# A larger fixed price for each VectorE instruction in the planner of a two-layer attention and S4D kernel, with later entries for the softmax inverses

## Chip, cores and metric

The kernel runs on one core of a Trainium2 chip. The metric is device time in microseconds (us) for one launch, as the median of several runs; for the kernel before it is 2675.46 us (three runs, 2673.86 to 2678.34).

## What is computed

The reference applies four residual layers to one sequence of 2048 rows of 640 float32 numbers: attention, S4D convolution, attention, S4D convolution, each with a layernorm in front, and with the same weights in both attentions and in both convolutions.

```python
def _A_ref(x, wqkv, wo):                      # 32 heads of 20
    q, k, v = split(x @ wqkv)
    p = softmax(einsum("bhqd,bhkd->bhqk", q, k) * 20 ** -0.5)
    return merge(einsum("bhqk,bhkd->bhqd", p, v)) @ wo

def _B_ref(u, log_A_real, A_imag, C_real, C_imag, log_dt, D_skip):
    ...
    K = 2.0 * einsum("dn,dnl->dl", C, exp(A * dt * pos)).real   # 640 x 2048, N = 128
    y = irfft(rfft(u_t, 4096) * rfft(K, 4096))[..., :2048]
    return y + u * D_skip

x = x + _A_ref(layernorm(x), ...);  x = x + _B_ref(layernorm(x), ...)   # twice
```

The convolution kernel K does not depend on x. It is built once, in pieces, beside the first attention, and used in both S4D layers.

## The kernel before

**Stages.** Attention 1 (its exponentials run from 116 to 1102 us of the span), its output projection and the transform of K, S4D 1, attention 2 (1491 to 2471 us), its output projection (2472 to 2523 us), S4D 2.

**A turn.** An attention goes through 32 turns: 8 groups g of 4 heads, and for each 4 blocks qb of 512 query rows. A turn walks over 16 tiles of 128 keys with two halves each, so it has 32 exponentials. `scores` (L851) issues eight small matmuls S (L858) into a PSUM tile of 128x1024 and one ScalarE exponential pt<-S; `values` (L884) issues eight matmuls pa (L892) for each key tile, which sum pt times V over the turn. V has a column of ones, so a row of each head's result is the softmax's sum. At a turn's last tile, `values` has VectorE copy pa0 into oc and add pa1 to it, and then multiply the oc of the turn before by db, the spread inverse of its sums (`scale`).

**The inverses.** Between a turn's end and that multiply, the sums go out to DRAM (dn<-oc, `sums`), come back spread over 128 partitions (dr<-dn, `load`), are inverted on VectorE (`invert`: a max and a reciprocal of 128x16), go out again (dn<-dr, `back`) and come back broadcast to all rows of a head (db<-dn, `spread`). These DMAs are issued from POOL's queue. Three more entries in the same list issue loads of kpw (DRAM to SBUF, also from POOL's queue), the tables from which K's next 32 channels are built.

**The filler.** `kgen` (L192 to L396) builds K. For each of 20 groups of 32 channels it has an expansion (28 small VectorE instructions on kpw, ktab, kwc, kwb, the last three of them ktab 128x896 and kdif 128x512), left parts (kat and ka, six VectorE instructions of 128x512) and right parts (kb), matmuls (L329) and evacuations of their sums (ko). Besides the filler there are jobs: projections to q and k (matmuls L611, evacuated by a group of five VectorE instructions qc, qc, sq, qhi, qlo) and to V (L577), a group of heads ahead. In the second attention there are pieces of its output projection instead of the filler (`rows_out`, L1040: pieces of three or two of a row's five tiles of 128, L1067), as many as fit; what is left of it is done after the attention by `out_proj` (L1286; matmuls L1307 and L1312).

**What sets the order.** The program is written out by a planner. `Plan` (L51) carries three running times, plan.pe, plan.act and plan.dve, while instructions are written. `Ordered.call` (L74) wraps every VectorE instruction: it adds a fixed part and elements/960 to plan.dve (which never stands more than 0.9 behind plan.pe), and ties the instruction behind the one written before it, so that VectorE's, POOL's and SyncE's (SP's) orders are those of the writing. Some decisions read these times:

- `fill` (L970), called for each exponential, first issues a tile's `values` when its exponentials are due, then jobs, then entries of `later` that are due, then filler.
- `weave` (L412) writes filler steps as long as plan.dve < plan.pe + 0.2.
- `emptied` (L404) puts an evacuation on VectorE not before plan.pe + 0.25, and marks the PSUM buffer free at plan.dve + 0.15; `slot` (L706) places a job's next matmuls only when its buffer is free.
- `later` is a list of (time, action): an action is issued when plan.pe has reached its time. The entries of the inverses are put at plan.dve plus an offset.
- `end_jobs` (L944) runs in the first turn in which the jobs are through; it finishes the filler and issues `prefetch` (L1147: the halves of wo, then x) from SP's queue.

So a VectorE instruction that is priced too low lets more filler be written ahead of the next evacuation than VectorE gets done by then; one that is priced too high holds filler back.

Of the kernel before, what the change touches and what calls it, by code (L numbers as in the profile page):

```python
# [62 lines left out]
class Ordered:  # L63
# [5 lines left out]
    def __getattr__(self, name):  # L69
        f = getattr(self.engine, name)  # L70
        if name not in ("dma_start", "memset", "partition_all_reduce", "activation", "copy") and not self.count:
            return f

        def call(out, *a, **k):  # L74
            if self.count:
                big = a[0].shape if "reduce" in name else out.shape
                self.plan.dve = max(self.plan.dve, self.plan.pe - 0.9) + 0.07 + math.prod(big[1:]) / 960
            made = f(out, *a, **k)  # L78
            if self.plan.keep:
                self.last = self.tie(made, self.last)  # L80
            elif self.floor is not None:
                self.tie(made, self.floor)
            return made
        return call
# [3 lines left out]
def mha_s4d_kernel(ctx, tc, x_in, wqkv, wo, lar, aim, cr, ci, ldt, dsk,  # L88
                   c_e1, c_eb, c_f2, c_fa, c_sel, c_lv, c_id, c_sg, c_e16, c_f16, c_id16, c_dn, out, parts="asas", general=None):
    nc = tc.nc  # L90
    plan = Plan()
# [97 lines left out]
    def chain(ins):  # L189
        last[0] = tie(ins, last[0])  # L190
# [208 lines left out]
    pend, slow = [], []  # L399
# [23 lines left out]
    def attention(x, stats):  # L423
# [100 lines left out]
        sqs, outs, later, ends = [[], []], [], [], [0.0, 0.0]  # L524
# [342 lines left out]
        def store_block(oc, blk):  # L867
            g, qb = divmod(blk, 4)
            for j in range(4):
                h = 4 * g + j  # L870
                ge.dma_start(ot[h * DH:(h + 1) * DH, 512 * qb:512 * qb + 512], oc[32 * j:32 * j + DH, :])
            stored[blk] = plan.pe

        def at_once(oc, blk):

            pb = pst("M", [P, 512], F32, tag="m0", name="m0")
            db = ev.tile([P, 512], F32, bufs=1, name="db")
            te.matmul(pb, dsel[0], oc, start=True, stop=True)
            ve.tensor_scalar_max(db, pb, 1e-30)
            ve.reciprocal(db, db)  # L880
            ve.tensor_mul(oc, oc, db)
            store_block(oc, blk)

        def values(qb, g, kt, pts, pa):  # L884

            V = Vt[g // 2 % 3]
            plan.on_pe(0.865)
            for r in range(2):
                rows = slice(64 * r, 64 * r + 64)
                for j in range(4):  # L890
                    h = 4 * (g % 2) + j
                    chain(te.matmul(pa[r][32 * j:32 * j + 32, :], V[rows, kt, VP * h:VP * h + 32],  # L892
                                    pts[j // 2][rows, 512 * (j % 2):512 * (j % 2) + 512],
                                    start=(kt == 0), stop=(kt == NI - 1), tile_position=(64 * r, 32 * j)))
            if kt == NI - 1:
                blk = 4 * g + qb
                oc = ev.tile([P, 512], F32, name="oc")
                dr = ev.tile([P, 16], F32, name="dr")
                db = []
                rows = dn[0, blk].rearrange("(j c) f -> j (c f)", j=4)  # L900
                plan.dve = max(plan.dve, plan.pe + 0.25)
                ve.tensor_copy(oc, pa[0])
                ve.tensor_add(oc, oc, pa[1])
                sums_[0] = plan.dve + 0.15
                while scaled:
                    scaled.pop(0)()
                if dsel and blk == NBK - 1:
                    later.append((plan.dve, lambda: at_once(oc, blk)))
                    return

                def sums():
                    for j in range(4):
                        ge.dma_start(rows[j:j + 1, :], oc[32 * j + DH:32 * j + DH + 1, :])

                def load():
                    ge.dma_start(dr, dn[0, blk])

                def invert():
                    ve.tensor_scalar_max(dr, dr, 1e-30)
                    ve.reciprocal(dr, dr)  # L920

                def back():
                    ge.dma_start(dn[1, blk], dr)

                def spread():
                    rows = dn[1, blk].rearrange("(j c) f -> j (c f)", j=4)
                    db.append(ev.tile([P, 512], F32, bufs=1, name="db"))
                    for j in range(4):
                        ge.dma_start(db[0][32 * j:32 * j + 32, :], rows[j:j + 1, :].to_broadcast([32, 512]))

                def scale():
                    ve.tensor_mul(oc, oc, db[0])
                    later.append((plan.dve + 0.3, lambda: store_block(oc, blk)))
                    later.sort(key=lambda e: e[0])
                later.extend((plan.dve + n, f) for n, f in (
                    (0.2, sums), (5.0, load), (10.0, invert), (11.0, back), (15.5, spread)))
                later.extend((plan.dve + n, lambda: slow and slow.pop(0)[1]()) for n in (18.0, 21.0, 24.0))
                if first_layer or g < H // 4 - 2:
                    scaled.append(scale)
                else:  # L940
                    later.append((plan.dve + 27.0, scale))
                later.sort(key=lambda e: e[0])
# [27 lines left out]
        def fill(j):  # L970

            if ready:
                t = max(ready[0][0] + 0.15, 0.0 if ready[0][3] else sums_[0])
                if t <= plan.pe + 0.1 or j and len(ready) > 2:
                    plan.on_pe(0.0, t)
                    values(*ready.pop(0)[1:])
            while slot(plan.act - 0.5):
                pass
            drain_later()
            weave()  # L980
# [146 lines left out]
        for r_ in ready:  # L1127
            values(*r_[1:])
# [574 lines left out]
```

## Time and profile before

| | |
|---|---|
| median of three runs | 2675.46 us (2673.86 to 2678.34) |
| profiled execution | 2680.85 us, its span 2679.1 us, mean granted TensorE clock 0.996 |
| TensorE (PE) busy | 2530.0 us, 94% |
| ScalarE (ACT) busy | 2368.7 us, 88% |
| VectorE (DVE) busy | 1516.0 us, 57% |
| GpSimd (POOL) busy | 827.7 us, 31% |
| 2048 exponentials pt<-S | 1928.6 us, 1032 ns each in the records, with ends that overlap the next one's start |
| exponentials of attention 1, first start to last end | 986 us |
| exponentials of attention 2 | 980 us |
| largest idle time of ACT before an exponential in attention 1 | 4.78 us, at 138.03 us |

In the prediction a row of the timeline reads: start, duration, engine, line, operation, out<-in, shapes, how many such instructions the row holds, and in brackets how long the engine stood idle before it and whose end it waited for. All VectorE and ScalarE instructions carry line 78 because the wrapper issues them; they are told apart by tile names. A row of the view by windows reads: window, its length, then the busy time and number of instructions on PE, PEld (weight load), DVE, ACT and POOL, then the granted clock as a share, the DMA share and GB/s. A row of grouped waits reads: engine, what waited, the releaser, and then us in total, number of times, longest.

### The profile page before, as it was taken

To read this page: it belongs to the slowest core of one execution; us is meant where nothing else is said; L and a number is where in the kernel's file an instruction comes from. 1 tells how busy PE (TensorE), PEld (TensorE's weight loads), DVE (VectorE), ACT (ScalarE), POOL (GpSimd) and SP (SyncE) were. 2 spreads that over 40 slices of the span, in tenths; PEclk is the share of its full clock that TensorE was granted. 3 is DMA by queue.
4 is the path that set the end of the run, shared out by engine and by line. 5 is a ranking of instruction groups with operands and counts; after the bars stand their busy time and mean duration, and the time that the engine had idled before them with its cause. 6 is when DMAs were issued, how large, how long until landed. Compare 5 with 4: busy or idle time off the path is not lost.

```text
span 2679.1 us, 116332 instructions
## 1 busy us (share of the span) xinstructions
PE 2530.0 (94%) x51106; PEld 1425.0 (53%) x51106; DVE 1516.0 (57%) x3451; ACT 2368.7 (88%) x2793; POOL 827.7 (31%) x1256
## 2 busy tenths in 40 slices
PE   7899999999999998899998999999999998999898
PEld 3445444444444443678896444454444443444788
DVE  8687777886855994477776333232233221154865
ACT  7889999999999999676655799999999999999564
POOL 1123323333323334301672122222222222222376
PEclk9999999999999999999999999999999999999999
DMA  6513222322221224364542121121121113222465
GB/s 210 181 49 86 67 76 55 87 55 76 52 61 49 54 68 155 110 233 162 189 151 69 40 59 50 50 58 47 45 65 38 54 30 93 69 67 60 145 190 162
DMA packets 186580, 242.18 MB, mean 90 GB/s; under 512 B 43376, under 2 KB 128976, under 8 KB 184400
## 3 DMA queue, kind: packets, MB, share of 16 engines
q1 hardware_dynamic: 150048, 188.35, 21.8%
q0 software_dynamic: 36016, 46.30, 7.0%
q8 instruction: 403, 6.60, 1.0%
q14 instruction: 113, 0.93, 0.1%
HBM read 158.50 MB, written 76.01 MB: 88 GB/s over the span
## 4 chain that ended last, share of the span: by engine, by line
ACT 52%; PE 25%; issue 10%; DVE 6%; DMA 3%; POOL 1%; SPq 0%; ACTq 0%; DVEq 0%; POOLq 0%
ACT pt L78 50%; PE pa L892 4%; PE psv L1419 3%; PE psy L1429 3%; PE S L858 3%; PE psx L1407 2%; PE m L611 1%; PE psx L1384 1%; PE po L1312 1%; DMA kop<-ks 1%; PE pst L1394 1%; PE pkf L1272 1%; DVE ktab L78 1%; PE po L1307 1%; PE pq L764 1%
## 5 line engine op out<-in xcount | busy, mean ns | idle before, releaser
L78 ACT ACTIVATE pt<-S 128x1024 f32<-128x1024 f32 x2048 | 1928.6, 1032 | 41.4 <-PE S L858 29.2
L892 PE MATMUL pa<-pt,V 64*32 64x512 f32 x16384 | 1100.9, 590 | 1.4 <-DVE oc L78 1.2
L858 PE MATMUL S<-qop,kop 61*32 61x512 f16 x16384 | 882.9, 381 | 85.2 <-ACT pt L78 68.4
L858 PEld LDWEIGHTS <-kop 61*32 61x32 f16 x16384 | 366.7, 89 | 741.1 <-issue 622.4
L892 PEld LDWEIGHTS pa<-pt,V 64*32 64x32 f32 x16384 | 315.1, 106 | 74.6 <-issue 9.7
L78 POOL DMA_DIRECT2D dn<-oc x252 | 124.5, 501 | 670.6 <-DVE oc L78 643.8
L78 DVE TENSOR_SCALAR qc<-m 128x512 f32<-128x512 f32 (+1 forms) x68 | 46.8, 689 | 303.6 <-PE m L611 303.6
L78 POOL DMA_DIRECT2D db<-dn x252 | 128.0, 514 | 135.1 <-DMA dn<-dr 132.1
L78 DVE COPY oc<-pa 128x512 f32<-128x512 f32 x64 | 44.1, 690 | 199.6 <-PE pa L892 191.9
L611 PE MATMUL m<-xh,wh 64*32 64x512 f16 x2560 | 147.9, 379 | 5.5 <-DVE qc L78 5.5
L78 POOL DMA_DIRECT2D ot<-oc x256 | 130.4, 516 | 71.6 <-DVE oc L78 42.8
L611 PE MATMUL m<-xh,wl 64*32 64x512 f16 x2560 | 148.1, 377 | 0.0
L611 PE MATMUL m<-xl,wh 64*32 64x512 f16 x2560 | 146.7, 376 | 0.0
L611 PEld LDWEIGHTS <-wh 64*32 64x32 f16 x5120 | 92.9, 93 | 78.4 <-issue 36.4
L78 ACT COPY xt<-pst 128x1024 f16<-128x1024 f16 x80 | 81.6, 1022 | 47.2 <-PE pst L1394 47.0
L1412 POOL TENSOR_TENSOR t<-t,kb 128x512 f32<-128x512 f32 x80 | 102.0, 1276 | 67.6 <-DVE t L78 66.7
L78 POOL DMA_DIRECT2D dn<-dr x63 | 35.3, 560 | 248.8 <-DVE dr L78 236.4
L78 DVE TENSOR_SCALAR V<-m 128x160 f32<-128x160 f32 x64 | 20.7, 324 | 158.5 <-PE m L577 158.5
L78 DVE TENSOR_TENSOR kb<-ktab 128x512 f32<-128x512 f32 x160 | 107.7, 692 | 0.0
L577 PEld LDWEIGHTS <-xh 128*128 128x128 f16 x960 | 79.7, 98 | 47.0 <-issue 31.6
L1413 POOL TENSOR_TENSOR t<-t,t 128x512 f32<-128x512 f32 x78 | 99.3, 1273 | 8.5 <-DVE t L78 2.6
L329 PEld LDWEIGHTS m<-kb,ka 128*32 128x32 f32 x3840 | 61.0, 109 | 72.1 <-issue 55.3
(305 smaller groups left out, 4020.7 us busy)
## 6 DMA issues: line engine op xcount, KB each, us to landing
ka<-kha SPq DMA_DIRECT2D x80, 256.0 KB
kb<-khb SPq DMA_DIRECT2D x80, 256.0 KB
db<-dn POOLq DMA_DIRECT2D x252, 64.0 KB, 2.6
kop<-ks SPq DMA_DIRECT2D x176, 80.0 KB
kpw<-wd POOLq DMA_DIRECT2D x60, 192.0 KB, 4.7
qop<-qs SPq DMA_DIRECT2D x256, 40.0 KB
ot<-oc POOLq DMA_DIRECT2D x256, 40.0 KB, 3.0
kha<-kn SPq DMA_DIRECT2D x20, 512.0 KB
```

What stands on the lines that cost most here:

```text
L78: made = f(out, *a, **k)
L329: chain(te.matmul(ps[32 * j:32 * j + 32, c8, :], a[n][:, ch, :], b[n][:, dd, :], start=(n == 0), stop=(n == 2), tile_position=(0, 32 * j)))
L577: chain(te.matmul(ps[:, :n], a_[:, ct, sl], m[:, ct, :], start=(k == 0), stop=(k == 14)))
L611: chain(te.matmul(ps[r][32 * t:32 * t + 32, :], a_[rows, ct, 32 * u:32 * u + 32], m[rows, ct, 512 * v:512 * v + 512], start=(k == 0), stop ...
L764: te.matmul(pq, a_[:, ct, :], m[:, ct, sl], start=(n == 0), stop=(n == 14))
L858: chain(te.matmul(S[32 * t:32 * t + 32, 512 * r:512 * r + 512], kt_[rows, kc + 32 * t:kc + 32 * t + 32], qt[rows, :], start=True, stop=Tru ...
L892: chain(te.matmul(pa[r][32 * j:32 * j + 32, :], V[rows, kt, VP * h:VP * h + 32], pts[j // 2][rows, 512 * (j % 2):512 * (j % 2) + 512], sta ...
L1407: te.matmul(px, f2[:, f, :], xt[:, k, :], start=(n == 0), stop=(n == 2))
L1412: ge.tensor_mul(t2, t2, kb)
L1413: (ge if g0 else ve).tensor_add(t1, t1, t2)
L1419: te.matmul(pv[:, g].rearrange("p r i c -> p (r i c)"), t1[:, g * P:g * P + P], fa, start=True, stop=True)
L1429: te.matmul(py[:, i, :], eb[:, 4 * i4 + i, r, :], v[:, r, 4 * i4 + i].rearrange("p g c -> p (g c)"), start=(r == 0), stop=(r == 1))
```

## The change

The fixed part in the planner's price of a VectorE instruction goes from 0.07 to 0.11 us, and the later entries of a turn's inverse (invert, back, spread and the three kpw loads) get larger offsets. No instruction computes anything else than before; the order in which they are written changes.

```diff
@@ class Ordered, call
-                self.plan.dve = max(self.plan.dve, self.plan.pe - 0.9) + 0.07 + math.prod(big[1:]) / 960
+                self.plan.dve = max(self.plan.dve, self.plan.pe - 0.9) + 0.11 + math.prod(big[1:]) / 960
...
@@ values, at a turn's last key tile
                 later.extend((plan.dve + n, f) for n, f in (
-                    (0.2, sums), (5.0, load), (10.0, invert), (11.0, back), (15.5, spread)))
-                later.extend((plan.dve + n, lambda: slow and slow.pop(0)[1]()) for n in (18.0, 21.0, 24.0))
+                    (0.2, sums), (5.0, load), (12.5, invert), (13.5, back), (18.0, spread)))
+                later.extend((plan.dve + n, lambda: slow and slow.pop(0)[1]()) for n in (20.5, 23.0, 25.5))
```

Three places show how the order moves. The numbers behind the names are the program's buffer numbers and differ between the two.

VectorE around the end of turn 1 of attention 1 (the 66th of its exponentials), before: the tail of an expansion (kwb, ktab, kdif) and the first left part (kat), then the evacuation of the turn (oc<-pa0, oc<-oc,pa1) and the multiply of the turn before.

```order
L78 TENSOR_TENSOR kwb0_2944<-ktab_1341 128x288
L78 TENSOR_TENSOR kwb1_2945<-ktab_1341 128x288
L78 TENSOR_TENSOR ktab_1341<-kwb0_2944,kwb1_2945 128x32x3x3
L78 TENSOR_TENSOR ktab_1341<-ktab_1341 128x896
L78 TENSOR_TENSOR kdif_1340<-ktab_1341 128x512
L78 TENSOR_TENSOR kat_3041<-ktab_1341 128x512
L78 COPY oc_3062<-pa0_2144 128x512
L78 TENSOR_TENSOR oc_3062<-oc_3062,pa1_2145 128x512
```

The same place in the changed program:

```order
L78 TENSOR_TENSOR kwb0_2979<-ktab_1341 128x288
L78 TENSOR_TENSOR kwb1_2980<-ktab_1341 128x288
L78 COPY oc_3054<-pa0_2143 128x512
L78 TENSOR_TENSOR oc_3054<-oc_3054,pa1_2144 128x512
L78 TENSOR_TENSOR oc_2189<-oc_2189,db_2763 128x512
L78 TENSOR_TENSOR ktab_1341<-kwb0_2979,kwb1_2980 128x32x3x3
L78 TENSOR_TENSOR ktab_1341<-ktab_1341 128x896
L78 TENSOR_TENSOR kdif_1340<-ktab_1341 128x512
L78 TENSOR_TENSOR kat_3182<-ktab_1341 128x512
```

The evacuation now stands ahead of the last ktab instructions, kdif and kat.

VectorE at the end of turn 6 (the 226th exponential), before: the end of a run of left and right parts, a group that evacuates a projection (qc to qlo), and the turn's evacuation.

```order
L78 TENSOR_TENSOR kb0_7337<-ktab_1341 128x512
L78 TENSOR_TENSOR kb1_7338<-ktab_1341,kdif_1340 128x512
L78 TENSOR_SCALAR qc_7371<-m0_7061 128x512
L78 SCALAR_TENSOR_TENSOR qc_7371<-m1_7062,qc_7371 128x512
L78 TENSOR_TENSOR sq_7374<-qc_7371 128x512
L78 CAST qhi_7375<-qc_7371 128x512
L78 TENSOR_TENSOR qlo_7376<-qc_7371,qhi_7375 128x512
L78 COPY oc_7399<-pa0_6449 128x512
L78 TENSOR_TENSOR oc_7399<-oc_7399,pa1_6450 128x512
```

The same evacuation in the changed program, with an expansion's first, smaller instructions ahead of it:

```order
L78 TENSOR_TENSOR kpw0_166<-kpw0_166 128x384
L78 COPY ktab_1341<-kpw0_166 128x32x3x2
L78 COPY ktab_1341<-kpw0_166 128x32x3
L78 COPY ktab_1341<-k_ci_173 128x32
L78 TENSOR_TENSOR kwc0_7311<-kpw0_166,k_cr_172 128x96
L78 TENSOR_TENSOR kwc1_7312<-kpw0_166,k_ci_173 128x96
L78 TENSOR_SCALAR ko_6011<-m1_7275 128x128
L78 COPY oc_7361<-pa0_6470 128x512
L78 TENSOR_TENSOR oc_7361<-oc_7361,pa1_6471 128x512
```

The projection's group no longer stands directly ahead of it, and the filler has come less far.

TensorE at the end of attention 2, before: the last piece of the output projection inside the attention (m, L1067, here its second half of three tiles), the broadcast of the last block's sums (L878), then `out_proj` (po), which begins with a piece of two tiles (x2 in each half's L1307 row).

```order
L1067 MATMUL m1_54315<-woh_49513,ol_54129 128x320
L1067 MATMUL m1_54315<-woh_49513,oh_54128 128x320
L1067 MATMUL m1_54315<-wol_49514,oh_54128 128x320
L878 MATMUL m0_54335<-oc_54310,dsel_30882 128x512
L1307 MATMUL po_54403<-woh_49513,ol_54392 128x320 x2
L1307 MATMUL po_54404<-woh_49513,ol_54392 128x320 x2
```

The same place in the changed program, where that last piece has two tiles:

```order
L1067 MATMUL m1_54292<-woh_49513,ol_54249 128x320
L1067 MATMUL m1_54292<-woh_49513,oh_54248 128x320
L1067 MATMUL m1_54292<-wol_49514,oh_54248 128x320
L878 MATMUL m0_54310<-oc_54281,dsel_30882 128x512
L1307 MATMUL po_54370<-woh_49513,ol_54359 128x320 x2
L1307 MATMUL po_54371<-woh_49513,ol_54359 128x320 x2
```

Counted over the whole attention, 37 tiles of rows are projected inside attention 2 before, and 36 after; seven rows are whole at its end before, six after. `out_proj` then has one piece of two tiles, two of three and seven rows of five before (43 tiles in 10 pieces), and one, four and six after (44 tiles in 11 pieces). The inverses in both attentions move a few places back in VectorE's and POOL's order; the filler's last matmuls in attention 1 stand at the 971st of its 1024 exponentials instead of the 953rd, and the prefetch of wo and x stands one turn later.

## The prediction, made before the changed kernel ran

> **What bounds the kernel now.** I read the chain that ended last, then the windows of the two attentions and of the second output projection, then ScalarE's idle times inside the attentions.
>
> ```profile
> ACT 52%; PE 25%; issue 10%; DVE 6%; DMA 3%; POOL 1%; SPq 0%; ACTq 0%; DVEq 0%; POOLq 0%
> 115.00:1102.00 987.00, 937.33 (x24322) 451.16 (x24327) 716.23 (x1532) 963.29 (x1026) 325.38 (x544) 1.00 0.26 71
> 1491.00:2472.00 981.00, 940.97 (x21195) 449.07 (x21187) 295.72 (x652) 966.82 (x1025) 232.84 (x456) 1.00 0.19 55
> 2472.00:2523.00 51.00, 44.68 (x328) 42.34 (x317) 44.05 (x123) 19.96 (x32) 14.46 (x15) 1.00 0.38 121
> 779.00:809.50 30.50, 29.91 (x700) 14.97 (x699) 7.23 (x14) 30.28 (x33) 7.67 (x15) 1.00 0.13 32
> L78 ACT ACTIVATE pt<-S 128x1024 f32<-128x1024 f32 x2048 | 1928.6, 1032 | 41.4 <-PE S L858 29.2
> ```
>
> More than half of the chain is ScalarE, nearly all of it the 2048 exponentials. In attention 1 ScalarE is busy 963 of 987 us and in attention 2 967 of 981, and TensorE 937 and 941: both run close to full, ScalarE ahead. In the quiet stretch from 779 to 809.5 us, 33 exponentials take 30.28 us, 0.92 us each, so 1024 of them need some 940 us. The change cannot touch that floor; it can only take away or add times in which ScalarE waits. All such waits before exponentials sum to 41.4 us in the two attentions, 29.2 of them for S. VectorE is busy 716 of 987 us in attention 1, where the filler is, and only 296 of 981 in attention 2. What an attention loses to VectorE is lost where VectorE comes late with something that TensorE waits for, so that the next S is late. These are ScalarE's rows in attention 1 where that happens.
>
> ```profile
> 138.03 1.02 ACT L78 ACTIVATE pt<-S 128x1024 f32<-128x1024 f32 x1 [4.78 <-PE S L858]
> 190.29 4.85 ACT L78 ACTIVATE pt<-S 128x1024 f32<-128x1024 f32 x5 [1.93 <-PE S L858]
> 300.73 2.10 ACT L78 ACTIVATE pt<-S 128x1024 f32<-128x1024 f32 x2 [0.84 <-PE S L858]
> 342.71 2.11 ACT L78 ACTIVATE pt<-S 128x1024 f32<-128x1024 f32 x2 [1.13 <-PE S L858]
> 345.91 2.10 ACT L78 ACTIVATE pt<-S 128x1024 f32<-128x1024 f32 x2 [1.09 <-PE S L858]
> 438.36 2.11 ACT L78 ACTIVATE pt<-S 128x1024 f32<-128x1024 f32 x2 [0.47 <-PE S L858]
> 441.56 4.09 ACT L78 ACTIVATE pt<-S 128x1024 f32<-128x1024 f32 x4 [1.09 <-PE S L858]
> 546.24 3.02 ACT L78 ACTIVATE pt<-S 128x1024 f32<-128x1024 f32 x3 [0.43 <-PE S L858]
> ```
>
> The row at 138.03 follows the first expansion, which waits for its table; VectorE's order there is the same after the change, so its 4.78 us stay. The other seven are 1.93 + 0.84 + 1.13 + 1.09 + 0.47 + 1.09 + 0.43 = **6.98 us**, all in the first half of the stage, and in each VectorE had been working without a break. Two of them in full: VectorE before the row at 190.29, with its chain, and before the row at 342.71.
>
> ```profile
> 184.65 0.46 DVE L78 TENSOR_TENSOR ktab<-kwb,kwb 128x288 f32<-128x288 f32 x1
> ...
> 186.15 0.68 DVE L78 TENSOR_TENSOR kdif<-ktab 128x512 f32<-128x512 f32 x1
> 186.75 0.69 DVE L78 TENSOR_TENSOR kat<-ktab 128x512 f32<-128x512 f32 x1
> 187.35 0.68 DVE L78 COPY oc<-pa 128x512 f32<-128x512 f32 x1
> 187.43 0.61 DVE oc L78
> 188.09 1.26 PE pa L892 x9
> 189.37 0.77 PE pa L892 x9
> 190.29 1.02 ACT pt L78
> 339.19 0.68 DVE L78 TENSOR_TENSOR kb<-ktab,kdif 128x512 f32<-128x512 f32 x1
> 339.79 0.68 DVE L78 TENSOR_SCALAR qc<-m 128x512 f32<-128x512 f32 x1
> 342.36 0.69 DVE L78 TENSOR_TENSOR qlo<-qc,qhi 128x512 f16<-128x512 f32 x1
> 342.98 0.68 DVE L78 COPY oc<-pa 128x512 f32<-128x512 f32 x1
> ```
>
> The turn's evacuation stands behind the expansion's tail; TensorE then has 18 pa matmuls to do before the next S, and ScalarE runs out. At 342.71 the evacuation stands behind a projection's group, and that behind left and right parts.
>
> **The change part by part.** First the price. An expansion is measured by this window, from its first kpw to its kbig:
>
> ```profile
> 123.75:133.48 9.73, 7.78 (x200) 3.48 (x185) 9.27 (x28) 9.50 (x11) 0.00 (x0) 1.00 0.03 9
> 123.77 0.56 DVE L78 TENSOR_TENSOR kpw<-kpw 128x384 f32<-128x384 f32 x1 [6.62 <-DMA kpw<-wd]
> 124.82 0.55 DVE L78 TENSOR_TENSOR kpw<-kpw 128x384 f32<-128x384 f32 x1
> 133.49 0.81 DVE L78 TENSOR_REDUCE kbig<-k_cr 128x1 f32<-128x640 f32 x1
> ```
>
> 28 instructions take 133.49 - 123.77 = 9.72 us. They have 5696 elements a partition, which the planner counts as 5.93 us; with 0.07 each it counts 7.89, with 0.11 it counts 9.01. So an expansion is short by 1.83 us before and by 0.71 after: about two exponentials before, less than one after. For wide instructions it is the other way: kdif, kat and oc above start every 0.60 us, and the planner counts 512/960 + 0.07 = 0.60 before and 0.64 after. A projection's group takes from 339.79 to 342.98, 3.19 us, against 3.02 counted before and 3.22 after. So the price becomes right for the expansions and the groups and 0.04 too high for left and right parts.
>
> [...]
>
> What the order makes of it, place by place. At 190.29 the evacuation moves ahead of the last two ktab instructions, kdif and kat, which take from 184.65 to 187.35, 2.7 us, against 1.93 of stall: gone. At 342.71 and 345.91 the group and the parts leave the place ahead of the evacuation (six or more instructions of 0.60 against 1.13 and 1.09): gone. At 438.36 and 441.56 the same pattern goes; at 300.73, where TensorE waits for a kb, and at 546.24, the filler now stands elsewhere. I count all 6.98. A new late place: the evacuation of turn 8, counted from 0, stands behind the last 24 instructions of an expansion and a wide one, 133.49 - 124.82 + 0.60 = 9.3 us of VectorE work written beside nine exponentials, 9 x 0.92 = 8.3 us, and the planner's slack of 0.2; it is some 0.8 late, and I put **+0.6** for it, since a little is made up for. The other 30 evacuations have room in the new order.
>
> Held-back filler costs nothing by itself: VectorE has 987 - 716 = 271 us idle in attention 1, and the filler's last matmuls move by 18 exponentials, 17 us, and end some 50 exponentials before the stage does. With it wo and x are asked for a turn (30 us) later on SP, behind a turn's operand loads, and the conversion of wo on POOL too. Attention 1 has a turn and more left then, and I put 0 (at worst the few us by which x could be late).
>
> The inverse is now 2.5 us later in each turn (invert, back, spread, kpw). What waits for it is the multiply, a turn after its evacuation:
>
> ```profile
> L78 DVE TENSOR_TENSOR oc<-oc,db 128x512 f32<-128x512 f32 x30 | 20.6, 685 | 1.6 <-DMA db<-dn 1.6
> DVE dr L78 <- DMA dr<-dn: 31.9, 11, 8.9
> ```
>
> Of 30 multiplies in attention 1, all but 1.6 us found db there, so 2.5 us mostly fit; below, at nothing, and above, at 1.6 us more in the worst turn, on an engine with idle time. The second row is what the later invert can give: VectorE stood 31.9 us at the head of its queue for dr in attention 1. Most of it hurt nobody (it is not on ScalarE's rows above), so I take 0 gain from it, and at most a few of the 41.4 - 4.78 - 6.98 = 29.6 us of waits of both attentions that are not listed above.
>
> In attention 2 the order of TensorE is the same until near the end; VectorE's rows move by a few places and none stands ahead of an evacuation that was late. I take 0 there. One tile less is projected inside (six matmuls) and one more behind it, in two pieces of three tiles more and a row of five less:
>
> ```profile
> 2478.47 3.35 DVE L78 RECIPROCAL db<-db 128x512 f32<-128x512 f32 x1
> 2509.39 1.73 PE po L1307 x10
> 2511.11 2.93 PE po L1312 x20
> 2506.82 0.48 DVE L78 TENSOR_TENSOR x<-x,po 128x320 f32<-128x320 f32 x1
> 2508.51 0.83 DVE L78 TENSOR_TENSOR ol<-otl,oh 128x640 fp32r<-128x640 f32 x1 [0.44 <-ACT oh L78]
> ```
>
> Six of such matmuls are 6 x 2.93/20 = 0.9 us: **-0.9** inside attention 2, where its end is TensorE's, and +0.9 behind it. There VectorE, busy 44.05 of 51 us, is nearly as full as TensorE (44.68), and gets two more adds of 0.48, one more ol (three fifths of 0.83) and one more row's layernorm (two statistics of 0.49 and small ones), 2.5 to 3 us together, of which a part falls beside the reciprocal's 3.35 us or a wait. So the stage gains between 0.9 (TensorE alone) and a whole row's 1.73 + 2.93 = 4.7; I take **+2.0**, near TensorE's end since the row moved is a fraction of a row.
>
> Sum: -6.98 + 0.6 - 0.9 + 2.0 = -5.3 us. Against the profiled execution, 2680.85 us (span 2679.1), that is 2675.6. The profiled one lies 5.4 above the median of the runs, 2675.46; from that median the same step gives **2670.2 us**.
>
> **The rivals.**
>
> *More goes than I count (20%).* The waits for loads and the small ones also shrink, since filler no longer runs ahead everywhere:
>
> ```profile
> PE S L858 <- DMA qop<-qm: 1.5, 3, 0.6
> PE S L858 <- DMA kop<-ks: 1.3, 1, 1.3
> ```
>
> These 2.8 us and some 2 of the 29.6 not listed would be 5 us more, -10, **2665 us**. For it: later kpw loads collide less with operand loads. Against it: nothing in the order of SP's loads changed at these places.
>
> *The old price was right for what matters (18%).* The wide instructions, at 0.60, say so, and by that the stalls come from elsewhere, such as the matmuls' own time: then the order changes, the stalls stay in kind at other exponentials, and what is left is the end of attention 2: -0.9 + 2.0 = +1.1, **2676.6 us**. The expansion's 9.72 us speaks against it.
>
> *Slower (22%).* The seven stalls are accidents of where 20 expansions and some 30 evacuations meet, and the new order has new meetings. An expansion is still short by 0.71 us, and 20 of them by 14 in all; one meeting costs up to 1.9 us (the row at 190.29). If eight evacuations or projections now come late by 1.2 us on average, that is +9.6, and with -6.98 and the end of attention 2 at its upper price (-0.9 + 4.7) it gives +6.5, **2682 us**. By that upper price it is slower than before from three such meetings on (6.98 - 3.8 = 3.2 us), and by over 5.4 us from eight. For it: the new meeting in turn 8, and TensorE's 95% in the stage, which leaves little to catch up with. Against it: I followed the order around each evacuation and found one.
>
> **How the numbers follow.** The forecast has 40%, with its own range -9 to -2. A measurement of this kernel can tell about 0.2%, 5.4 us, from no change, and the forecast lies on that border: 22% of its 40 fall beyond it and 18 within. Faster by over 0.2%: 0.22 + 0.20 = 0.42. Within: 0.18 and most of the second rival's, 0.16, = 0.34. Slower: 0.22 and 0.02 = 0.24. The range reaches from the first rival with 2 us of spread, 2663, to the slower one's, 2682.
>
> **What would show it.** In the changed profile the seven rows of idle ScalarE in the first half of attention 1 should be gone and one of about 0.6 us be found near 405 us, at the evacuation of turn 8; the stage should be 980 us, not 986. Attention 2 should take its 980 us again, a tenth of a per cent less, and the stage behind it 53 us instead of 51. I am wrong if the stage of attention 1 has as many waits for S at other places (then expansions still come late), if a wait for db appears before a multiply and TensorE behind it, or if x is late after attention 1.

## The result, and the profile after

The changed kernel is slower: a median of 2684.07 us (seven runs, 2682.38 to 2687.05) against 2677.56 us of the kernel before in seven runs on the same chip, a ratio of 1.0028 with a 95% interval of 1.0016 to 1.004, which is 4 to 11 us. The forecast was 5.3 us faster. The profiled execution took 2684.27 us, its span 2682.5; the one of before, 2680.85 us, lies 3.3 above that kernel's median, so the two spans differ by only 3.4 us, and the lengths below account for those.

The chain that ended last, the windows of the two attentions and of what follows the second, and the group of the exponentials, all of the changed kernel:

```profile
ACT 57%; PE 21%; issue 11%; DVE 4%; DMA 2%; POOL 1%; SPq 0%; ACTq 0%; POOLq 0%; DVEq 0%
115.00:1102.00 987.00, 934.65 (x24328) 446.12 (x24327) 713.93 (x1532) 961.52 (x1025) 323.40 (x544) 0.99 0.25 71
1491.00:2472.00 981.00, 940.67 (x21182) 449.20 (x21188) 289.73 (x632) 966.38 (x1025) 230.97 (x456) 1.00 0.19 55
2472.00:2526.00 54.00, 46.93 (x332) 43.98 (x327) 45.84 (x128) 22.58 (x38) 16.29 (x16) 0.98 0.40 125
L78 ACT ACTIVATE pt<-S 128x1024 f32<-128x1024 f32 x2048 | 1927.6, 1034 | 33.3 <-PE S L858 21.5
```

ScalarE's waits before exponentials fell from 41.4 to 33.3 us, those for S from 29.2 to 21.5: about what was forecast. Yet attention 1 is as long as it was. The view of one tile gives its length: first and last start of the 1024 exponentials of attention 1 (first row of each) and of attention 2, of the kernel before,

```profile
L78 ACT ACTIVATE pt<-S x1024: 1009/1025/1087, 115.8 to 1100.8; 128x1024 f32<-128x1024 f32 x171
L78 ACT ACTIVATE pt<-S x1024: 1017/1025/1086, 1491.2 to 2470.4; 128x1024 f32<-128x1024 f32 x171
```

and of the changed one:

```profile
L78 ACT ACTIVATE pt<-S x1024: 1016/1024/1088, 114.5 to 1100.3; 128x1024 f32<-128x1024 f32 x171
L78 ACT ACTIVATE pt<-S x1024: 1017/1024/1087, 1491.9 to 2470.8; 128x1024 f32<-128x1024 f32 x171
```

First start to last start, attention 1 went from 985.0 to 985.8 us, the stretch between the attentions from 390.4 to 391.6, attention 2 from 979.2 to 978.9, and what follows it, to the end of the span, from 208.7 to 211.7. With the start, 1.3 us earlier, that is the 3.4 us.

Where the seven stalls stood, ScalarE's timeline of the changed kernel now has unbroken rows, and at 400.74 us one small new stall (the evacuation of turn 8):

```profile
179.87 20.71 ACT L78 ACTIVATE pt<-S 128x1024 f32<-128x1024 f32 x22
294.66 10.48 ACT L78 ACTIVATE pt<-S 128x1024 f32<-128x1024 f32 x11
337.21 13.16 ACT L78 ACTIVATE pt<-S 128x1024 f32<-128x1024 f32 x14
400.74 11.43 ACT L78 ACTIVATE pt<-S 128x1024 f32<-128x1024 f32 x12 [0.47 <-PE S L858]
433.73 13.25 ACT L78 ACTIVATE pt<-S 128x1024 f32<-128x1024 f32 x14
539.75 10.38 ACT L78 ACTIVATE pt<-S 128x1024 f32<-128x1024 f32 x11
```

What took the gain back is in the last turn of attention 1, in a row that is no exponential. ScalarE, changed kernel:

```profile
1059.21 8.55 ACT L78 ACTIVATE pt<-S 128x1024 f32<-128x1024 f32 x9
1077.37 0.72 ACT L78 CAST oh<-otl 128x640 fp32r<-128x640 f32 x1 [9.61 <-DMA otl<-ot]
1078.00 3.76 ACT L78 ACTIVATE pt<-S 128x1024 f32<-128x1024 f32 x4
1082.87 18.54 ACT L78 ACTIVATE pt<-S 128x1024 f32<-128x1024 f32 x20 [1.11 <-PE S L858]
```

and before:

```profile
1069.76 9.47 ACT L78 ACTIVATE pt<-S 128x1024 f32<-128x1024 f32 x10
1079.11 0.73 ACT L78 CAST oh<-otl 128x640 fp32r<-128x640 f32 x1
1079.72 22.11 ACT L78 ACTIVATE pt<-S 128x1024 f32<-128x1024 f32 x24
```

The conversion oh<-otl of the output projection's second row stands in ScalarE's order 24 exponentials ahead of the end, in both kernels. Before, ScalarE came to it at 1079 us and the load was there. After, it came 11 us earlier and stood 9.61 us, with all exponentials behind it. Why the load was not there, from SP's queue, its waits, POOL's rows and the chain that ended last, all of the changed kernel:

```profile
1034.46 2.47 SPq L78 DMA_DIRECT2D wot<-in_wo  x5
1059.98 0.38 SPq L78 DMA_DIRECT2D otl<-ot  x1
1060.41 1.48 SPq L78 DMA_DIRECT2D x<-in_x_in  x3
1061.93 0.44 SPq L78 DMA_DIRECT2D otl<-ot  x1
```

```profile
SPq L78 <- POOL wol L1170: 16.2, 1, 16.2
```

```profile
1039.64 1.39 POOL L1169 CAST woh<-wot 128x640 fp32r<-128x640 f32 x2
1048.59 3.04 POOL L1170 TENSOR_TENSOR wol<-wot,woh 128x640 fp32r<-128x640 f32 x2 [7.56 <-issue]
1058.41 1.54 POOL L1170 TENSOR_TENSOR wol<-wot,woh 128x640 fp32r<-128x640 f32 x1
```

```profile
1061.93 15.19 DMA otl<-ot
```

The prefetch issued wo at 1034.46 (1015.13 before). POOL split it into halves from 1039.64 to 1059.95, and the buffers of the row loads lie where wo was staged, so SP waited 16.2 us for POOL. Then it issued one row load, three x loads of 1.28 MB, and the second row load, which landed 15.19 us after its issue, at 1077.12 (the last row is from the chain).

In the kernel before, SP issued both row loads behind the x loads, at nearly the same time:

```profile
1057.53 1.31 SPq L78 DMA_DIRECT2D x<-in_x_in  x3
1059.15 0.99 SPq L78 DMA_DIRECT2D otl<-ot  x2
```

The second went out at 1059.58 and the trace has its last landing at 1074.92 us, 15.3 us later and 4.2 us before ScalarE came to the conversion. In the changed kernel it landed only 2.2 us later, and ScalarE came 11.4 us earlier: the attention had run ahead, and the load had not moved with it.

### The profile page after: what moved, and what is told of

Its sections match the earlier page's. It is cut to its first block, busy times and chain, and to the rows that moved or that the text cites. A ratio compares the mean times of both kernels' runs of the same rounds, so it can differ in the third digit from the quotient of the medians.

```text
span 2682.5 us, 116314 instructions
## 1 busy us (share of the span) xinstructions
PE 2527.8 (94%) x51106; PEld 1421.3 (53%) x51106; DVE 1508.4 (56%) x3435; ACT 2369.5 (88%) x2796; POOL 825.7 (31%) x1257
## 4 chain that ended last, share of the span: by engine, by line
ACT 57%; PE 21%; issue 11%; DVE 4%; DMA 2%; POOL 1%; SPq 0%; ACTq 0%; POOLq 0%; DVEq 0%
ACT pt L78 56%; PE psy L1429 3%; PE psv L1419 3%; PE pa L892 2%; PE psx L1407 2%; PE S L858 1%; PE psx L1384 1%; PE po L1312 1%; PE pkf L1272 1%; PE pst L1394 1%; PE po L1307 1%; PE m L611 1%; DMA otl<-ot 1%; PE pq L764 1%; PE pkt L1264 1%
## 5 line engine op out<-in xcount | busy, mean ns | idle before, releaser
L78 ACT ACTIVATE pt<-S 128x1024 f32<-128x1024 f32 x2048 | 1927.6, 1034 | 33.3 <-PE S L858 21.5
```

## The experiments

Theory A says that the change shortens attention 1 by 8 to 10 us, that the late prefetch takes 9.6 us back through one load that one conversion waits for, and that the tile moved behind attention 2 costs 3 us. Rivals: B, the transition's transfers are late in any case, so the loss would only move; C, the 3 us at the end are scatter; others stand with their runs. The lengths below are read as above, each from one profiled execution (us; "tail" is from attention 2's last start to the span's end). Each ratio is to the kernel before on the same chip; E1 to E4, E5 to E8 and E9 to E12 ran on three different chips.

| kernel | ratio to before, 95% | attention 1 | attention 2 | tail |
|---|---|---|---|---|
| before | 1 | 985.0 | 979.2 | 208.7 |
| changed | 1.0028 (1.0016 to 1.004) | 985.8 | 978.9 | 211.7 |
| E1 both row loads first | 0.9997 (0.9988 to 1.0006) | 977.0 | 982.3 | 211.6 |
| E2 change in attention 1 alone | 1.0019 (1.001 to 1.0028) | 989.3 | 979.0 | 208.4 |
| E3 change in attention 2 alone | 1.0007 (0.9998 to 1.0016) | 983.9 | 978.4 | 211.6 |
| E4 = E1 and E2 | 0.9991 (0.9982 to 1.0) | 977.3 | 982.8 | 208.8 |
| E5 before, only the prefetch late | 1.0069 (1.0055 to 1.0083) | 997.0 | 981.7 | 209.6 |
| E6 changed, conversion late | 0.9978 (0.9969 to 0.9987) | 975.6 | 977.9 | 214.7 |
| E7 changed, one more copy | 1.0029 (1.0017 to 1.0042) | 987.9 | 979.1 | 212.9 |
| E8 = E4 and one more copy | 0.9997 (0.9987 to 1.0006) | 978.5 | 985.0 | 208.4 |
| E9 = E2 and E6 | 0.9968 (0.9955 to 0.9981) | 976.5 | 979.8 | 208.6 |
| E10 price alone, conversion late | 0.9978 (0.9969 to 0.9987) | 974.9 | 977.5 | 214.4 |
| E11 = E4 and two more copies | 0.9974 (0.9963 to 0.9985) | 977.1 | 979.8 | 208.5 |
| E12 offsets alone | 1.0028 (1.0019 to 1.0037) | 991.8 | 979.3 | 208.5 |

**E1, both row loads ahead of x.**

```diff
-                                  (plan.pe + 21.0, lambda: rows.load(rows.left.pop(0)))))
+                                  (plan.pe + 7.2, lambda: rows.load(rows.left.pop(0)))))
```

> The changed kernel with one entry moved: the second load of the output projection's rows (otl) is issued right behind the first, ahead of the three x loads of 1.28 MB, instead of behind them. Theory A (attention 1 did get about 10 us faster, and gave 9.6 us back where ScalarE stood for this load in its last turn): the row of 9.6 us idle before oh<-otl goes, attention 1 takes 977 us instead of 987, and the time is about 2674.5 us. Rival B (the first load comes too late in any case, because it waits for POOL's conversion of wo, and what is won is met by another transfer of the transition, x or kl): the stop stays or moves to the adds of x, and the time stays at 2682 to 2685 us.

Attention 1 took 977.0 us. SP's and ScalarE's rows in E1:

```profile
1063.12 0.95 SPq L78 DMA_DIRECT2D otl<-ot  x2
1064.11 1.48 SPq L78 DMA_DIRECT2D x<-in_x_in  x3
```

```profile
1059.73 10.38 ACT L78 ACTIVATE pt<-S 128x1024 f32<-128x1024 f32 x11
1070.00 0.73 ACT L78 CAST oh<-otl 128x640 fp32r<-128x640 f32 x1
```

The loads went out at 1063 us, later than in the changed kernel, the second landed at 1068.26, and the conversion at 1070 did not wait. So it was the x loads ahead of it in SP's queue that delayed the load: behind them it took 15.19 us from issue to landing, ahead of them at most 7 (issued at 1063, converted at 1070). Rival B falls. The DMA engines were full over that stretch of the changed kernel (share 1.01 of their time from 1061 to 1077 us, 363 GB/s):

```profile
1061.00:1077.00 16.00, 6.66 (x144) 2.51 (x129) 2.07 (x3) 6.76 (x8) 5.48 (x11) 0.90 1.01 363
```

The two runs show what the place in the queue does to this load; how the DMA engines share their work among queued copies they do not show. The time came to 0.9997 instead of the expected 0.9988 (2674.5 beside 2677.6), some 2.4 us short: attention 2 took 982.3 us, 3.4 more than in the changed kernel, though nothing in it was edited. E7, E8 and E11 are about that.

**E2 and E3, the change in one attention alone.** The price becomes a variable of the plan, and price and offsets follow the layer:

```diff
+        first_layer = stats is None; late = first_layer; plan.price = 0.11 if late else 0.07
...
-                    (0.2, sums), (5.0, load), (12.5, invert), (13.5, back), (18.0, spread)))
+                    (0.2, sums), (5.0, load), (12.5 if late else 10.0, invert), (13.5 if late else 11.0, back), (18.0 if late else 15.5, spread)))
```

(E3 has `late = not first_layer`.)

> The change's price and offsets in attention 1 alone; attention 2 is planned as before. Theory A: attention 1 as in the changed kernel (987 us with the stop of 9.6 us for otl), the output projection behind attention 2 as before, about 3 us shorter than in the changed kernel: 2681 us. Rival C (the change loses its time in attention 1 alone, and the 3 us at the end are scatter): 2684 us, as the changed kernel.

> The change's price and offsets in attention 2 alone; attention 1 is planned as before. Theory A: attention 1 as before (986 us), the output projection behind attention 2 some 3 us longer: 2680 to 2681 us, against 2677.6 of before. Rival C: no change against before.

E2's time, 1.0019, lies below the changed kernel's 1.0028 as theory A has it, but the two intervals overlap. The tails tell more: E2's is 208.4 us and E3's 211.6. Over all profiles, the eight with `out_proj` planned as before have tails of 208.4 to 209.6 us, the six with 11 pieces 211.6 to 214.7: the 3 us are no scatter, and rival C falls. E3's whole time, 1.9 us over before with an interval that takes in no change, would not have shown it alone. The spread within the six goes with the clock: over the first 60 us of the tail the granted clock was 0.97 in the kernel before, the changed one, E1, E3 and E9, 0.94 in E7 (212.9) and 0.92 in E6 and E10 (214.7 and 214.4). E2 has the stop before the conversion again (10.74 us).

**E4, E1 and E2 together.**

> The change in attention 1 alone, and the second otl load ahead of the x loads. Theory A: the sum of the two experiments before it, 9.6 us less of the stop and 3 us less at the end than the changed kernel, about 2671.5 us, 6 us faster than before. Rival B: 2679 to 2682 us.

The ratio is 0.9991, some 2.4 us faster than before instead of 6, with an interval that reaches to no change; 3.6 us stand in attention 2 (982.8 against 979.2), as in E1.

**E5, nothing but the prefetch a turn later.**

```diff
-            if tail is None and filler[0] is None and have.issuperset(every):
+            if tail is None and filler[0] is None and have.issuperset(every) and (n >= 30 or not first_layer):
```

> The kernel before, with nothing changed but the prefetch of wo and x, which is issued a turn later (behind turn 30 instead of 29, counted from 0); VectorE's, TensorE's and ScalarE's orders are those of before. Theory A (the late prefetch alone makes the load otl late, by POOL's 25 us of conversion and the x loads ahead of it): ScalarE stands some 5 to 9 us before oh<-otl in the last turn, and the time is 5 to 9 us over that of before. Rival D (the prefetch has room, and the stop came only because attention 1 ran ahead of its transfers by 10 us): ScalarE stands under 2 us there, and the time is that of before, within 2 us.

```profile
1073.91 0.38 SPq L78 DMA_DIRECT2D otl<-ot  x1
1074.34 1.47 SPq L78 DMA_DIRECT2D x<-in_x_in  x3
1075.85 13.14 SPq L78 DMA_DIRECT2D otl<-ot  x2
```

```profile
1088.30 0.72 ACT L78 CAST oh<-otl 128x640 fp32r<-128x640 f32 x1 [13.24 <-DMA otl<-ot]
```

In the order of before, with all its stalls, the late prefetch alone stops ScalarE for 13.24 us and costs 0.69%, some 18 us. (The last SP row holds a further load, issued at 1088.6; the one that ScalarE waits for landed at 1088.20, 13.3 us later than in the kernel before.) So rival D falls as it was put: the prefetch had no such room. Theory A's own size was too small: the stop is longer than in the changed kernel, because POOL finished wo at 1073.9 here, 14 us later, while ScalarE came to the conversion only 7 us later; and attention 2 shows the stops of E1 and E4 too (981.7), though the loads were not exchanged here. What E5 does not show is the reverse, the new price with the prefetch in its old place. In the changed kernel the load landed only 2.2 us later than before, so how much of the 9.61 us would have stayed there, because attention 1 runs ahead, is open.

**E6, the conversion behind the last exponential, loads as they are.**

```diff
-        se.floor = None if first_layer else se.last
+        se.floor = se.last
```

> The changed kernel, with the ScalarE conversion oh<-otl of the output projection's second row held behind the attention's last exponential, instead of among the last turn's; the loads stay as they are. Theory A: the stop of 9.6 us goes from attention 1 (977 us), the output projection begins at most 1 us later on its second row, and the time is about 8 us under that of the changed kernel, about the same as before. Rival B (the transfers of the transition are late in any case): the 9.6 us turn up in the output projection instead, where the first adds wait for x or otl, and the time stays.

```profile
1063.46 28.96 ACT L78 ACTIVATE pt<-S 128x1024 f32<-128x1024 f32 x31
1092.24 0.78 ACT L78 CAST oh<-otl 128x640 fp32r<-128x640 f32 x1
```

The exponentials run through, attention 1 takes 975.6 us, and the time is 0.9978, 6 us under before, where theory A had expected none; against the changed kernel the two intervals leave a gain of 8 to 19 us, and 8 was expected. With the conversion its own 0.7 us and the 1.11 us of waiting four exponentials behind it (1.01 in E1, which has no stop) have also left the row of exponentials. Nothing turned up in the output projection in its place: the stretch between the attentions is 392.0 us against 391.6.

**E7, E8 and E11, the stops in attention 2.** In E1 ScalarE's waits in attention 2 have a row that names ScalarE itself as the releaser (8 of the 16 stops are long enough for it), and its timeline shows one:

```profile
ACT pt L78 <- ACT pt L78: 2.2, 8, 0.3
```

```profile
1536.03 4.69 ACT L78 ACTIVATE pt<-S 128x1024 f32<-128x1024 f32 x5 [0.22 <-ACT pt L78]
```

They stand at every 64th exponential. Counted in the traces, with the instructions that only wait, the first exponential of attention 2 is ScalarE's instruction number 2777 (counted from 0) in E1, E4, E5 and E8, which have the stops, and an even number, 2776 to 2780, in the other ten, which have none. The copies were to shift that number:

```diff
+        [se.copy(sm.tile([P, 1], F32, name="nul"), x[:, 0, 0:1]) for _ in range(1 * (not first_layer))]
```

> The changed kernel with one more ScalarE instruction (a copy of 128x1 that nothing reads) during S4D 1. In the runs with both loads first, attention 2 took 3.4 to 3.8 us more in the same order of instructions: ScalarE stood some 0.2 us at one exponential in each 64, always the same one, and the number of ScalarE's instructions ahead of attention 2 was odd there and even elsewhere. Theory E (it is the place of the exponentials in ScalarE's instruction stream): this copy makes the number odd, the 16 stops appear here too, and attention 2 takes 983.5 us instead of 980. Rival F (the stops belong to the transfers' times after the loads were exchanged): attention 2 takes 980 us, the time is that of the changed kernel.

> The change in attention 1 alone, the second load ahead of the x loads, and the additional copy during S4D 1. Theory E: the number of ScalarE's instructions ahead of attention 2 is even again, the 16 stops go, attention 2 takes 980 us, and the time is 3.5 us under the same kernel without the copy, some 6 us faster than before (a ratio of 0.9978). Rival F: attention 2 takes 983.8 us and the ratio stays at 0.999.

> The change in attention 1 alone with both loads first, and two copies of 128x1 on ScalarE during S4D 1 (one copy left the number of ScalarE's instructions as it was, since it took over the wait of another instruction). Theory E (place in the instruction stream): the first exponential of attention 2 stands one place later, at an even place, the 16 stops of 0.2 us go and attention 2 takes 980 us instead of 984; the ratio is 0.998 instead of 0.999. Rival F (the transfers' times): the stops stay and attention 2 takes 984 us.

One copy tested nothing, and theory E's numbers for E7 and E8 missed: the copy took over the wait of another instruction, which went, and the numbers stayed 2776 (E7) and 2777 (E8, with the stops). With two the number is 2778, the row is gone, and attention 2 takes 979.8 us instead of E4's 982.8; the ratio goes from 0.9991 to 0.9974, on another chip and with intervals that overlap. So the stops follow the place in ScalarE's stream, and rival F falls, by E11 and by E5. What happens at that place the traces do not show.

**E9, the best of these: the change in attention 1 alone and the late conversion.**

> The change in attention 1 alone, with the conversion oh<-otl behind the attention's last exponential. Theory A: attention 1 takes 977 us, attention 2 980 us, the stretch behind attention 2 is 207.6 us as before instead of 210.7; the ratio to before is about 0.9967, some 9 us faster (2.7 us more than with the conversion moved in the changed kernel, 0.9978). Rival C (the 3 us at the end are scatter): the ratio stays at 0.9978.

It takes 2673.34 us against 2680.37, a ratio of 0.9968 (0.9955 to 0.9981): faster than the kernel before by 5 to 12 us, and than the changed one.

**E10 and E12, price and offsets apart.** E10 is the price alone with E6's line, E12 the offsets alone.

> The price 0.11 alone, in both attentions, with the old offsets of the inverses, and the conversion oh<-otl behind the last exponential (which takes the stop for otl out of the comparison). Theory A (the stalls of VectorE go by the price; the offsets do little): attention 1 takes 976 to 979 us, and the ratio is that of both edits with the same conversion, 0.9978 within 0.001. Rival G (the offsets hold the gain, since the inverses no longer stand ahead of evacuations): attention 1 takes 983 us or more, and the ratio is 1.000 or over.

> The later offsets alone, with the old price 0.07. Theory A: the prefetch stays where it is before, no stop for otl appears, the stalls of attention 1 stay for the most part: attention 1 takes 983 to 988 us and the ratio is 0.999 to 1.001. Rival G (the offsets hold the gain): attention 1 takes 979 us or less, and the ratio is 0.997.

E10 is E6 without the offsets and has the same ratio, 0.9978 (each to about 0.001): rival G falls, the gain is the price's, and beside the new price the offsets add nothing that these runs can tell. E12 missed theory A's numbers: with the old price the offsets make attention 1 6.8 us longer. Of ScalarE's rows, the first here is an old stall, the second an old one that grew from 1.09, the third a new one in turn 12:

```profile
341.99 2.11 ACT L78 ACTIVATE pt<-S 128x1024 f32<-128x1024 f32 x2 [1.14 <-PE S L858]
440.78 29.46 ACT L78 ACTIVATE pt<-S 128x1024 f32<-128x1024 f32 x31 [1.52 <-PE S L858]
500.16 10.56 ACT L78 ACTIVATE pt<-S 128x1024 f32<-128x1024 f32 x11 [3.31 <-PE S L858]
```

TensorE's waits in attention 1 name the loads of qop for 4.3 us in all (1.5 before). Behind the third stall the chain runs back from a load of qop (issued at 493.08, landed at 499.50) over SP's issues to a projection's qhi, which VectorE reached at 479.62 only, after an expansion's last rows, kat and ka: a projection that came late. Why the offsets bring this about with the old price and not with the new one stays open.

## Why the prediction was wrong

- **The floor and the seven stalls** were read rightly. All seven rows are gone. The stall of 4.78 us at the first expansion, which was to stay, is 2.90 us here, but it varies from run to run: it is 3.21 us in E3, whose attention 1 is that of before. One stall that the forecast did not list grew: ScalarE's wait while TensorE waits for a load of q, 1.25 us at 372.77 before, is 2.82 us at 366.21. Where nothing stops the last turn (E1, E4, E6, E8 to E11), attention 1 takes 974.9 to 978.5 us against 985.0 and, in E3, 983.9 (E6, E9 and E10 are also rid of the conversion there): 5 to 10 us less, where 6.4 were forecast with the new stall.
- **The price of an expansion** as the cause: right, by E10. The second rival (the old price right, stalls staying) is out for this kernel.
- **The new stall**, forecast with 0.6 us near 405 us, measured 0.47 at 400.74.
- **The step that failed** is this: "With it wo and x are asked for a turn (30 us) later on SP ... I put 0 (at worst the few us by which x could be late)." I looked for who needs x, and left out what else the prefetch issues and what stands behind it in SP's queue: the row loads otl, whose buffers wait for POOL's 20 us on wo, and which share the queue with x. And I left out that one reader of them, a conversion, stands inside the attention on the very engine that sets its end. In the kernel before that load landed 4.2 us ahead of its reader, so the room was not the turn and more that the forecast saw. ScalarE stood 9.61 us, and without the stop (E6) attention 1 is 10.2 us shorter, against a gain of 9.4 over the kernel before. E5 shows that the late prefetch by itself takes the room away; which share of the 9.61 us it has, and which the faster attention, stays open. ScalarE's row at 1079.11 in the profile of before would have told: an instruction that is no exponential, in the last turn, with a DMA's tile as its input.
- **The inverse 2.5 us later**: VectorE stood 5.3 us for db before one multiply, at 1068.55 us beside the x loads, more than I had allowed (1.6 us before, and 1.6 more at worst); E10, without the offsets, has a wait of 8.3 us before a multiply in the same turn, and TensorE's waits in attention 1 name no oc. By E10 the later inverse neither gains nor costs with the new price, by E12 it costs with the old one. The forecast of 0 held for the change as made.
- **The end**: -0.9 and +2.0 were forecast; attention 2 is 0.3 shorter (E3 0.8), the tail 3.0 longer, within the bounds of 0.9 to 4.7. About half is `out_proj` itself (1.5 us), the rest the first part of S4D behind it, where TensorE's waits for VectorE's x and for e1s grew by 1.6 us. Before:

```profile
PE psx L1384 <- DVE x L78: 3.3, 1, 3.3
PE psx L1384 <- DMA e1s<-in_c_e: 0.2, 1, 0.2
```

and changed:

```profile
PE psx L1384 <- DVE x L78: 4.0, 1, 4.0
PE po L1307 <- DVE ol L78: 1.8, 3, 1.4
PE psx L1384 <- DMA e1s<-in_c_e: 1.1, 1, 1.1
```

- **The slower rival** foresaw the sign by another mechanism (new late evacuations, eight of them). There was one, so its sign came out by luck; the 2684 us also lie above its 2682.

## What to carry to other kernels

A planner's number moves more than the instructions that it prices: list every step whose place depends on the moment when the filler is done, with each DMA that it issues, the queue in which it stands, and the first instruction that waits for it. A load that is small and needed soon goes ahead of large ones on the same queue (here 320 KB and three times 1.28 MB: 15.19 us to its landing behind them, at most 7 ahead of them), and a conversion that waits for a load does not belong among the instructions of the engine that bounds the stage; either remedy took the stop of 9.61 us away here (E1, E6). With the late conversion (E6) the kernel ends 6 us under the one before; with the loads first (E1) it ends level with it, since attention 2 then took 3.4 us more. Gains of less than a per cent are best looked for stage by stage, and with the granted clock beside each stage.

## What the runs showed of the hardware

- ScalarE stopped some 0.2 us (0.07 to 0.33) at every 64th exponential (with its semaphore instruction, every 128th instruction) when attention 2 began at an odd place of its stream, 3.0 us in E1, and not at an even one; one instruction more or less in an earlier stage decides it (E11).
- POOL stood 7.56 us before its first subtraction of wo (7.30 in the kernel before, 10.03 in E5), with nothing to wait for in the profile. What POOL did in that time no run here tested. The 7.56 us are over a third of the 20.3 us (1039.64 to 1059.95) that POOL took for wo, behind which the row loads waited.
